# W_out column sums by 64x32 tiles of TensorE, and batch 0 by column halves, in a fused attention and MLP kernel

## The chip, the core and the metric

The kernel runs on one core of one Trainium2 chip. The metric is the device time of one launch in microseconds (us), the median of several runs on the same chip. Engines are named as in the profile: PE is TensorE's matmul stream (PEld its weight loads), DVE is VectorE, ACT is ScalarE, POOL is GpSimd and SP is SyncE. POOL and SP issue the DMA transfers here. PSUM is the memory that PE writes into; DVE and ACT read it out ("evacuate" it).

## What is computed

Two attentions in a row, then a two-layer MLP. For each of 8 batches and 8 heads, 32 packed queries p attend over 576 keys; their result serves as both keys and values for the 576 queries q. The 8 heads of 64 are put side by side to give x, 4608 rows of 512.

```python
# q, k, v: (8, 8, 576, 64)   p: (8, 8, 32, 64)   all float32
def sm_attn(qq, kk, vv):
    s = scale * np.matmul(qq, kk.transpose(0, 1, 3, 2))
    s = s - np.max(s, axis=-1, keepdims=True)
    a = np.exp(s)
    a = a / (np.sum(a, axis=-1, keepdims=True) + 1e-09)
    return np.matmul(a, vv)
p_packed = sm_attn(p, k, v)
out = sm_attn(q, p_packed, p_packed)
# x: (4608, 512)   w_in: (512, 2048)   w_out: (2048, 512)   s, b: one number each
h = x @ w_in
r = np.maximum(h, 0.0)
g = s * (r * r) + b
return (g @ w_out).astype(np.float32)
```

Since g = s r² + b, the result is s (r² @ w_out) plus b times the column sums of w_out. The kernel computes r² @ w_out and the column sums apart, and joins them when a result tile leaves PSUM.

## The kernel before

A batch of 576 columns goes through these steps, each a function and, in the written order, a short word (the numbers behind a word are the batch and a part of the work):

- `k`, `kh`, `kf`, `q`, `qh`, `v`, `p`, `win`, `wout`: loads. Nearly all go through POOL's queue in the order in which they are written; batch 0's first half of k comes through SP in f32 and is cast by DVE and ACT (`kc`).
- `pT` (`prep_p`), `kT` (`prep_k`, by half of the heads), `qT` (`prep_q`, by half of the heads): transposes on PE into PSUM, copied out by DVE and, for half of q, ACT. From batch 3 on k and q are transposed by DMA on SP's queue (`qo`, `qD`, `kD`).
- `s` (`first_scores`, two words): the scores of p against k, and their exp on ACT (tile e1). `a` (`packed`, two words): exp times v, and the row sums; then DVE writes ppc (the packed result), rd (the reciprocal) and rs.
- `c` (`second_scores`): 16 products of ppc with q, and two exps on ACT (tile e2). `w` (`weights`, two words): the sums of e2 over the packed queries by a product with block ones, ln on ACT (tile ld), exp(-ln) on ACT (tile rcd), and a DVE product that gives the attention weights aT.
- `e` (`packed_w1`, four words) or `E` (`packed_w`, two words): ppc times W_in, scaled by rd, gives pw. The MLP's first layer is then only pw times aT, so attention's second product is never formed. Of an `e` word ACT scales one half and DVE the other.
- `m` (`mlp_in`, 16 words): four products of pw and aT (128x288 each), relu on ACT (tile rlu), square on DVE (into gT).
- `t` (`Out.step(2)`): two of the 16 accumulating products of gT with W_out of one result tile y. At a tile's last step DVE forms s·y + biasrep (tile ysb), and SP's queue stores it.

Batches 0 to 2, and batch 3 up to its weights, follow a list of words written out by hand (ORDER, lines 15 to 29). Every engine keeps its instructions in that order; PE, ACT and DVE each run through their own queue and wait for one another by semaphores. The remaining batches run in a loop of 16 steps (line 682 on) in which one m and several products of the batch before alternate.

PSUM gives four large buffers at first, in two rings of two (`ring`, line 89); the function `big()` takes the next one and waits until it has been evacuated. The word `four` (line 620) takes the two buffers of one ring for good: their four halves hold the three result tiles y[0], y[1], y[2] and the bias sum, and from there on `big()` has two buffers. The word `three` (line 625) gives up all of these and divides PSUM anew: three large buffers and two result tiles.

The column sums of W_out (`bias_part`, line 499) are 16 products of a 128x128 block of ones with W_out, accumulated in the fourth half, two at a time as the words b.0 to b.7; DVE multiplies them by b into biasrep. The lines:

```python
for m in range(m0, m1):
    mm(bps, onesb[:], w_out_sb[:, m, :], start=(m == 0), stop=(m == NFF - 1))
```

`mm` and `tr` (lines 92 to 96) wrap every matmul and transpose, and all DVE, ACT, POOL and SP instructions go through one helper (line 104). The profile's lines L93, L96 and L104 are these helpers, so its rows are told apart by tile names and not by lines.

Of the kernel before, what the change touches and what calls it, by code (L numbers as in the profile page):

```python
# [7 lines left out]
F32 = mybir.dt.float32  # L8
BF16 = mybir.dt.bfloat16
AF = mybir.ActivationFunctionType  # L10
ALU = mybir.AluOpType
# [1 line left out]


ORDER = """
kf kh.0.1 p.0.1 kc v.0 mask kT.0.0 qh.0.0 qh.0.1 pp2.0.1 kT.0.1 pT.0 win.0 s.0.0 s.0.1 a.0.0 win.2
qT.0.0 qT.0.1 p.1.2 a.0.1 c.0 w.0.0 e.0.0 win.1 win.3 wout.0 k.1 w.0.1 e.0.1 q.1 wout.1 e.0.2 m.0.3
pp2.1.2 m.0.0 e.0.3 wout.2 m.0.7 m.0.1 m.0.12 m.0.15 m.0.10 m.0.5 m.0.2 v.1 m.0.14 sb four b.0
kT.1.0 t.2 kT.1.1 t.1 m.0.4 qT.1.0 wout.3 b.1 qT.1.1 t.2 b.2 m.0.6 m.0.13 b.3 m.0.11 k.2 q.2 p.2.8
pT.1 t.0 t.1 t.0 b.4 s.1.0 t.1 s.1.1 t.2 m.0.8 b.5 a.1.0 m.0.9 a.1.1 b.6 t.0 c.1 b.7 t.0 t.1 q.3  # L20
kT.2.0 e.1.0 t.2 t.1 w.1.0 pp2.2.8 v.2 t.1 k.3 t.0 w.1.1 qT.2.1 t.0 t.1 t.0 t.0 e.1.1 t.2 kT.2.1 t.2
t.1 t.2 t.2 m.1.0 m.1.3 v.3 three t.3 t.3 pT.2 e.1.2 m.1.2 qT.2.0 t.3 t.3 m.1.1 m.1.5 m.1.7 t.3
e.1.3 m.1.9 qo.3 qD.3 kD.3 s.2.0 t.3 t.4 k.4 m.1.14 pT.3 t.4 m.1.4 s.2.1 t.3 m.1.13 m.1.15 m.1.6
m.1.8 t.4 m.1.11 m.1.10 m.1.12 a.2.0 t.4 t.4 t.3 a.2.1 t.4 t.4 c.2 t.5 t.4 t.5 q.4 E.2.0 t.6 t.5
w.2.0 t.6 w.2.1 s.3.0 t.5 pT.4 t.6 t.6 vo.3 s.3.1 t.5 t.5 m.2.2 m.2.3 t.6 E.2.1 m.2.1 t.6 t.5 v.4
a.3.0 t.5 m.2.5 a.3.1 t.6 m.2.0 t.7 m.2.15 qo.4 t.7 m.2.4 m.2.9 t.7 qD.4 m.2.7 t.7 c.3 t.7 t.6 m.2.6
kD.4 m.2.14 m.2.10 m.2.13 t.7 w.3.0 t.8 t.7 t.8 E.3.0 t.8 t.7 t.8 w.3.1 t.8 E.3.1 t.8 m.2.11 vo.4
t.8 t.8 m.2.12 m.2.8
"""

@with_exitstack
def kernel(
# [21 lines left out]
    B, H, S, D = q.shape  # L54
    NP = p.shape[2]
    DM = H * D
    DFF = moe_w_in.shape[1]
    P = 128
    scale = 1.0 / float(D) ** 0.5

    R = 96
    NC = S // R
    CP = NC // 2
    HP = H // 2
    NQ = H // 4
    NKC = DM // P
    NFF = DFF // P
    NB = 512
    NCH = DFF // NB
    HS = S // 2  # L70
# [21 lines left out]
    def mm(*a, **kw):  # L92
        return tc.keep_in_program_order(nc.tensor.matmul(*a, **kw))  # L93

    def tr(*a, **kw):
        return tc.keep_in_program_order(nc.tensor.transpose(*a, **kw))  # L96
# [11 lines left out]
    def big(dt=F32):  # L108
        w = NB if dt == F32 else 2 * NB
        rings["n"] += 1  # L110
        ps = rings["h"][rings["n"] % len(rings["h"])]
        return ps.tile([P, 2, w], dt, tag="h", name="hps")
# [10 lines left out]
    def raw(name, b):  # L123
        if (name, b - 1) in mine and b > 3:
            mine[name, b] = mine[name, b - 1]
        else:
            mine[name, b] = spare.pop(0)
        return bufs[mine[name, b]][:]
# [7 lines left out]
    def done(name, b):  # L136

        halves[name, b] = halves.get((name, b), 0) + 1
        if halves[name, b] == 2:
            give(name, b)  # L140
# [9 lines left out]
    def load_pairs(store, src, b, tag, half):  # L150

        if half == 0:
            store[b] = raw(tag, b).rearrange("r (h x) -> r h x", h=H)
        for h2 in range(2):
            h0 = HP * h2 + 2 * half
            pool.dma_start(
                out=store[b][:, h0:h0 + 2, :],
                in_=src[b, h0:h0 + 2].rearrange("h (r c) d -> r h (c d)", c=NC),
            )

    w_in_sb = wpool.tile([P, NKC, DFF], BF16, name="w_in_sb")
    w_out_sb = wpool.tile([P, NFF, NB], BF16, name="w_out_sb")
    gT = wpool.tile([P, NFF, 3 * S], BF16, name="gT")
# [51 lines left out]
    vec.memset(onesbd[:], 0.0)  # L215
    for g in range(4):
        vec.memset(onesbd[NP * g:NP * g + NP, NP * g:NP * g + NP], 1.0)
    onesb = constp.tile([P, P], BF16, name="onesb")
    vec.memset(onesb[:], 1.0)
    onesf = constp.tile([P, P], F32, name="onesf")  # L220
    vec.memset(onesf[:], 1.0)
    biasrep = constp.tile([P, NB], F32, name="biasrep")

    def idle(n):
# [60 lines left out]
    def prep_q(b, half):  # L285

        i = b % 2
        tp = big(BF16)
        for x in range(2):
            hp = 2 * half + x  # L290
            for c in range(NC):
                for h2 in range(2):
                    tr(
                        tp[D * h2:D * h2 + D, x, c * R:(c + 1) * R],
                        qn[b][:, hp + HP * h2, c * D:(c + 1) * D],
                        identb[0:R, 0:R],
                    )
        for x in range(2):
            dst = qT[i][:, :, 2 * half + x, :]
            src = tp[:, x, 0:S].rearrange("p (c r) -> p c r", c=NC)  # L300
            if x == 0:
                act.copy(out=dst, in_=src)
            else:
                vec.tensor_copy(out=dst, in_=src)
        done("qn", b)
# [107 lines left out]
    def weights(b, qd):  # L413
# [8 lines left out]
        act.activation(out=rcd[:], in_=ld[:].rearrange("p a s -> p (a s)"), func=AF.Exp, scale=-1.0)  # L422
        vec.tensor_tensor(out=aT[b][:, qd, :], in0=e2[b][:, qd, :], in1=rcd[:], op=ALU.mult)

    def packed_mm(i, ch, outs):

        for hp in range(HP):
            for h2 in range(2):
                mm(
                    outs[h2][NP * hp:NP * hp + NP, :],  # L430
                    ppc[i][D * h2:D * h2 + D, hp, :],
                    w_in_sb[D * h2:D * h2 + D, hp, ch * NB:(ch + 1) * NB],
                    start=True,
                    stop=True,
                    tile_position=(D * h2, NP * hp),
                )
# [32 lines left out]
    def slot(b):  # L469
        return 1 if b % 2 else (b % 4)  # L470
# [5 lines left out]
    def mlp_in(b, m, on_act=True):  # L476
        hps = big()
        for qd in range(NQ):
            for hf in range(2):
                mm(  # L480
                    hps[:, hf, 0:HS],
                    pw[b][:, qd, m * P:(m + 1) * P],
                    aT[b][:, qd, hf * HS:(hf + 1) * HS],
                    start=(qd == 0),
                    stop=(qd == NQ - 1),
                )
        g0 = slot(b) * S
        dst = gT[:, m, g0:g0 + S].rearrange("p (a s) -> p a s", a=2)
        if on_act:
            rlu = ysp.tile([P, 2, HS], BF16, tag="rlu", name="rlu")  # L490
            act.activation(out=rlu[:], in_=hps[:, :, 0:HS], func=AF.Relu)
            vec.tensor_tensor(out=dst, in0=rlu[:], in1=rlu[:], op=ALU.mult)
        else:
            vec.scalar_tensor_tensor(
                out=dst, in0=hps[:, :, 0:HS], scalar=0.0, in1=hps[:, :, 0:HS],
                op0=ALU.max, op1=ALU.mult,
            )

    def bias_part(bps, m0, m1):
        for m in range(m0, m1):  # L500
            mm(bps, onesb[:], w_out_sb[:, m, :], start=(m == 0), stop=(m == NFF - 1))
        if m1 == NFF:
            vec.tensor_scalar_mul(out=biasrep[:], in0=bps, scalar1=bvec[:])

    def sum_w_out(x):

        d = slice(NB // 8 * x, NB // 8 * (x + 1))
        vec.tensor_reduce(
            out=biasrep[:, d], in_=w_out_sb[:, :, d].rearrange("p m d -> p d m"),
            axis=mybir.AxisListType.X, op=ALU.add,  # L510
        )

    def bias_sum():

        bps = big()[:, 0, :]
        mm(bps, onesf[:], biasrep[:], start=True, stop=True)
        vec.tensor_scalar_mul(out=biasrep[:], in0=bps, scalar1=bvec[:])

    def store(ysb, i0, b, col, n, d=slice(0, NB), queues=(sp,)):
# [91 lines left out]


    y = outs(0) + outs(1) + outs(2)
    bias = {}

    def bias_step(x):

        bias_part(bias["ps"], 2 * x, 2 * x + 2)

    def four():  # L620
        ya, yb = (ring[1].tile([P, 2, NB], F32, tag="h", name="yps") for _ in range(2))
        y[0].yps, y[1].yps, y[2].yps, bias["ps"] = (t[:, x, :] for t in (ya, yb) for x in range(2))
        rings["h"] = ring[0:1]

    def three():
# [10 lines left out]
    def constants():  # L636
        sp.dma_start(out=svec[:], in_=moe_s[0:1].unsqueeze(0).to_broadcast([P, 1]))
        sp.dma_start(out=bvec[:], in_=moe_b[0:1].unsqueeze(0).to_broadcast([P, 1]))

    words = {  # L640
        "k": lambda b: load(kn, k, b, "kn"),
        "q": lambda b: load(qn, q, b, "qn"),
# [1 line left out]
        "kh": lambda b, x: load(kn, k, b, "kn", 4 * x, 4 * x + 4),  # L644
        "qh": lambda b, x: load_pairs(qn, q, b, "qn", x),
        "vh": lambda b, x: load_pairs(vn, v, b, "vn", x),
        "kf": load_first_k,
        "kc": cast_first_k,
        "p": lambda b0, b1: load_p(b0, min(b1, B)),
# [7 lines left out]
        "pp2": lambda b0, b1: twice_p(b0, min(b1, B)),  # L657
        "pT": prep_p,
        "kT": prep_k,
        "qT": prep_q,  # L660
        "kD": dma_k,
        "qo": order_q,
        "qD": dma_q,
        "vo": order_v,
        "s": first_scores,
        "a": packed,
        "c": second_scores,
        "w": weights,
        "e": packed_w1,
        "E": packed_w,  # L670
        "m": lambda b, m: mlp_in(b, m),
        "n": lambda b, m: mlp_in(b, m, False),
        "t": lambda t: y[t].step(2),
        "b": bias_step,
        "r": sum_w_out,
        "bs": bias_sum,
    }
    for word in ORDER.split():
# [3 lines left out]
    for b in range(3, B):  # L682
        a = b + 1
# [62 lines left out]
```

## Time and profile before

| | |
|---|---|
| median of 7 runs | 259.06 us (258.80 to 259.52) |
| the profiled execution: its time, its span | 258.96 us, 257.2 us |
| PE busy (share of the span), instructions | 237.1 us (92%), 2283 |
| DVE busy | 144.0 us (56%) |
| ACT busy | 145.0 us (56%) |
| POOL busy | 31.3 us (12%) |
| DMA, moved | 34.61 MB, mean 135 GB/s |
| PE busy in 0 to 25 us | 12.6 of 25 us |
| PE busy in 25 to 40 us | 13.7 of 15 us |
| PE busy in 40 to 100 us | 59.1 of 60 us |
| rlu (ACT), 128 instructions | 651 ns each |
| gT (DVE), 128 instructions | 457 ns each |
| pw of 512 columns, DVE / ACT | 750 / 684 ns each |
| first pw scaling of batch 0; its last gT square | starts at 22.14 us; at 46.43 us |

Times within the execution count from the span's start. "Busy" of PE is the union of its matmuls, each from its start to its modelled end; matmuls are pipelined, so the next one starts before the last has ended, and the time that a group costs is read from its start to the start of the next group. The bytes are counted as written: most loads read f32 and write bf16.

### The profile page before, as it was taken

Reading aid. Unit: us, or ns where it says so; the run is one execution under the profiler, and the core shown is the slowest. Engines: PE = TensorE matmul, PEld = TensorE weight load, DVE = VectorE, ACT = ScalarE, POOL = GpSimd, SP = SyncE. Lnnn points to the kernel's source line nnn. Section 1 sums busy time; section 2 is a strip of 40 time slices with the busy share of each in tenths; the row PEclk is TensorE's granted clock in tenths of the full one; section 3 lists DMA queues with packets and bytes.
Section 4 is the critical chain, followed back from the end, with each engine's and each line's share of the span. In section 5 each row is a group of like instructions: output and inputs, shape, how many; then the busy total and the mean of one; then the engine's idle time right before and its main releaser. Section 6 shows DMA issues by size and latency. Waiting matters only on the chain.

```text
span 257.2 us, 5569 instructions
## 1 busy us (share of the span) xinstructions
PE 237.1 (92%) x2283; PEld 138.0 (54%) x2320; DVE 144.0 (56%) x299; ACT 145.0 (56%) x220; POOL 31.3 (12%) x47
## 2 busy tenths in 40 slices
PE   1477889999999999999999999999999999999994
PEld 1362556555655664665566456655565555555443
DVE  3324753576765877857854668366835473444212
ACT  3038936456848688848763674568554764444000
POOL 8366230110002100300030003000000000000000
PEclk9999999999999999999999999999999999999999
DMA  5999999999398969993979398946611113111332
GB/s 110 183 203 204 204 206 205 197 200 247 71 161 131 176 133 162 157 233 81 186 99 219 99 177 122 235 90 133 136 43 41 43 41 87 41 41 41 84 82 82
DMA packets 54858, 34.61 MB, mean 135 GB/s; under 512 B 27568, under 2 KB 50352, under 8 KB 54832
## 3 DMA queue, kind: packets, MB, share of 16 engines
q0 software_dynamic: 24864, 18.32, 48.2%
q1 hardware_dynamic: 29872, 15.87, 27.3%
q8 instruction: 18, 0.29, 0.5%
q14 instruction: 8, 0.07, 0.1%
q10 hardware_dynamic: 96, 0.07, 0.1%
HBM read 37.23 MB, written 9.44 MB: 181 GB/s over the span
## 4 chain that ended last, share of the span: by engine, by line
PE 82%; DMA 13%; issue 2%; POOL 1%; ACT 1%; DVE 0%; ACTq 0%; POOLq 0%
PE yps L93 48%; PE hps L93 32%; DMA w_out_sb<-in_moe_w_out_dram 6%; DMA raw<-in_v_dram 4%; DMA w_in_sb<-in_moe_w_in_dram 3%; PE hps L96 1%; POOL raw L104 1%; ACT rlu L104 1%; DVE gT L104 0%; DVE ysb L104 0%; POOL pn L104 0%; ACTq L104 0%; POOLq L730 0%
## 5 line engine op out<-in xcount | busy, mean ns | idle before, releaser
L93 PE MATMUL yps<-w_out_sb,gT 128*128 128x512 bf16 (+2 forms) x558 | 138.3, 373 | 2.7 <-issue 1.4
L104 ACT ACTIVATE rlu<-hps 128x576 bf16<-128x576 f32 x128 | 80.7, 651 | 63.5 <-PE hps L93 57.6
L104 DVE TENSOR_TENSOR gT<-rlu 128x576 bf16<-128x576 bf16 x128 | 58.1, 457 | 62.1 <-ACT rlu L104 60.2
L93 PE MATMUL hps<-aT,pw 128*128 128x288 bf16 x512 | 81.0, 289 | 0.6 <-DVE pw L104 0.4
L93 PEld LDWEIGHTS <-gT 128*128 128x128 bf16 x592 | 53.2, 98 | 48.6 <-issue 6.4
L93 PEld LDWEIGHTS <-pw 128*128 128x128 bf16 x512 | 49.6, 98 | 34.1 <-issue 1.1
L104 DVE SCALAR_TENSOR_TENSOR ysb<-yps,svec,biasrep 128x512 f32<-128x512 f32 (+2 forms) x37 | 27.0, 732 | 16.6 <-PE yps L93 16.5
L104 DVE TENSOR_SCALAR pw<-hps,rd 128x1024 bf16<-128x1024 f32 (+1 forms) x20 | 21.3, 1067 | 1.9 <-ACT pw L104 1.4
L104 ACT ACTIVATE pw<-hps,rd 128x1024 bf16<-128x1024 f32 (+1 forms) x20 | 18.7, 941 | 4.1 <-PE hps L93 3.3
L104 DVE TENSOR_TENSOR aT<-e,rcd 128x576 bf16<-128x576 bf16 x16 | 12.1, 758 | 13.1 <-ACT rcd L104 13.1
L96 PE MATMUL hps<-identb,raw 96*64 96x96 bf16 (+1 forms) x216 | 9.9, 232 | 8.7 <-DVE raw L104 5.7
L104 POOL DMA_DIRECT2D raw<-in_k_dram x8 | 6.3, 790 | 93.3 <-DMA kT<-raw 83.7
L104 ACT ACTIVATE e<-hps 96x768 bf16<-96x768 f32 x16 | 12.6, 800 | 8.3 <-PE hps L93 8.3
L104 ACT ACTIVATE e<-hps,rs 128x576 bf16<-128x576 f32 x16 | 10.9, 737 | 6.4 <-PE hps L93 6.4
L96 PEld LDWEIGHTS <-raw 96*64 96x64 bf16 (+1 forms) x216 | 8.5, 123 | 11.1 <-DVE raw L104 5.7
L93 PE MATMUL hps<-w_in_sb,ppc 64*32 64x512 bf16 x256 | 11.8, 404 | 1.0 <-DMA w_in_sb<-in_moe_w_in_dram 1.0
L104 ACT ACTIVATE rcd<-ld 128x576 f32<-128x576 f32 x16 | 10.9, 683 | 0.5
L104 ACT ACTIVATE ld<-hps 128x576 f32<-128x576 f32 x16 | 10.3, 646 | 1.2 <-PE hps L93 1.0
L104 DVE COPY raw<-raw 96x1536 bf16<-96x1536 bf16 x20 | 10.4, 562 | 0.0
L93 PEld LDWEIGHTS <-raw 96*64 96x64 bf16 (+1 forms) x264 | 8.4, 113 | 2.9 <-issue 2.1
L93 PE MATMUL hps<-e,raw 96*64 96x32 bf16 (+1 forms) x264 | 9.1, 193 | 0.8 <-ACT e L104 0.8
L93 PE MATMUL hps<-pbd,kT 128*128 128x64 bf16 x192 | 8.6, 199 | 1.1 <-DVE pbd L104 1.1
(41 smaller groups left out, 97.1 us busy)
## 6 DMA issues: line engine op xcount, KB each, us to landing
raw<-in_v_dram POOLq DMA_DIRECT2D x8, 576.0 KB, 11.8
out_dram<-ysb SPq DMA_DIRECT2D x23, 192.0 KB, 2.6
raw<-in_k_dram POOLq DMA_DIRECT2D x7, 576.0 KB, 6.7
raw<-in_q_dram POOLq DMA_DIRECT2D x7, 576.0 KB, 10.5
out_dram<-ysb SPq DMA_DIRECT2D x24, 128.0 KB, 2.5
w_in_sb<-in_moe_w_in_dram POOLq DMA_DIRECT2D x8, 256.0 KB, 8.8
w_out_sb<-in_moe_w_out_dram POOLq DMA_DIRECT2D x4, 512.0 KB, 16.6
out_dram<-ysb SPq DMA_DIRECT2D x23, 64.0 KB, 2.2
```

The lines of the kernel that those rows point to most:

```text
L93: return tc.keep_in_program_order(nc.tensor.matmul(*a, **kw))
L96: return tc.keep_in_program_order(nc.tensor.transpose(*a, **kw))
L104: return lambda *a, **kw: tc.keep_in_program_order(f(*a, **kw))
```

## The change

- The words `b` go. In their place one word `B` (`sums_w_out`) forms all sums at one point: for each of 16 blocks of W_out and each half of the partitions one product of a 64x32 block of ones with 64 rows of W_out, on one of eight tiles of the array. 32 products leave partial sums in four groups of 32 partitions and two halves of one large buffer. DVE copies one half into biasrep and adds the other.
- The word `bs` (`bias_sum`, which was there and unused) forms one f32 product of biasrep with a 128x128 block of 1/32 (`parts`, which was `onesf`, a block of 1), and DVE multiplies by b.
- `four` gives the fourth half to y[3], so four result tiles of batch 0 are open.
- Batch 0 goes by column halves of 288: `prep_q_chunks`, `second_scores_half`, `weights_half` and `mlp_in_half` take 288 columns of all heads, or of two blocks of the MLP, where the old functions take 576 columns of half the heads, or of one block. The number of products and their sizes stay the same; the exps of batch 0's second scores are four of 288 columns in place of two of 576.
- Batch 0's W pieces, and one of batch 1, become `f` words: `packed_w1` with both halves on DVE.
- ORDER is written anew in all its lines. Four words `z` (one product of zeros, 128x512) stand near its start.

```diff
-kf kh.0.1 p.0.1 kc v.0 mask kT.0.0 qh.0.0 qh.0.1 pp2.0.1 kT.0.1 pT.0 win.0 s.0.0 s.0.1 a.0.0 win.2
-qT.0.0 qT.0.1 p.1.2 a.0.1 c.0 w.0.0 e.0.0 win.1 win.3 wout.0 k.1 w.0.1 e.0.1 q.1 wout.1 e.0.2 m.0.3
...
+kf kh.0.1 qh.0.0 mask kT.0.1 p.0.1 z kc z pp2.0.1 z qh.0.1 z kT.0.0 pT.0 v.0 qT.0.1 s.0.0 s.0.1
+qT.0.0 a.0.0 win.0 win.1 a.0.1 c.0.0 win.2 f.0.0 w.0.0 c.0.1 f.0.1 p.1.2 q.1 wout.0 w.0.1 h.0.2
+win.3 sb f.0.2 h.0.0 wout.1 k.1 h.0.4 h.0.3 h.0.8 h.0.6 h.0.10 h.0.1 h.0.9 four wout.2 pp2.1.2
+qT.1.0 t.1 h.0.5 t.0 t.1 t.2 t.2 h.0.7 t.3 wout.3 t.0 v.1 f.0.3 k.2 t.3 q.2 t.0 h.0.11 h.0.15 t.3
+h.0.14 t.2 t.3 t.1 h.0.12 t.0 kT.1.0 qT.1.1 t.3 t.2 pT.1 p.2.8 t.3 kT.1.1 B t.2 t.1 t.2 h.0.13 t.1
+k.3 s.1.0 s.1.1 t.1 t.3 bs t.1 a.1.0 kT.2.1 q.3 a.1.1 t.3 c.1 t.1 pp2.2.8 t.2 w.1.0 qT.2.0 t.2 w.1.1
+t.0 t.0 e.1.0 t.0 v.2 qT.2.1 t.0 m.1.0 three pT.2 kT.2.0 v.3 e.1.1 m.1.2 m.1.1 f.1.2 m.1.5 t.5 e.1.3
+m.1.3 t.4 m.1.8 m.1.4 t.4 qo.3 m.1.7 m.1.9 m.1.10 m.1.13 t.4 qD.3 m.1.15 m.1.6 m.1.14 s.2.0 t.5
+s.2.1 m.1.11 t.4 m.1.12 t.4 a.2.0 pT.4 kD.3 a.2.1 t.4 t.4 c.2 pT.3 t.4 t.5 E.2.0 t.5 w.2.0 k.4 t.5
...
-    onesb = constp.tile([P, P], BF16, name="onesb")
+    onesb = constp.tile([P, 32], BF16, name="onesb")
-    onesf = constp.tile([P, P], F32, name="onesf")
-    vec.memset(onesf[:], 1.0)
+    parts = constp.tile([P, P], F32, name="parts")
+    vec.memset(parts[:], 1.0 / 32)
...
+    def weights_half(b, hf):
+        cols = slice(hf * HS, (hf + 1) * HS)
+        dps = big()
+        for qd in range(NQ):
+            mm(dps[:, qd, 0:HS], onesbd[:], e2[b][:, qd, cols], start=True, stop=True)
...
+    def mlp_in_half(b, x):
+        mp, hf = divmod(x, 2)
+        hps = big()
+        for y in range(2):
+            m = 2 * mp + y
+            for qd in range(NQ):
+                mm(
+                    hps[:, y, 0:HS],
+                    pw[b][:, qd, m * P:(m + 1) * P],
+                    aT[b][:, qd, hf * HS:(hf + 1) * HS],
...
+    def sums_w_out():
+        t = big()
+        for g in range(4):
+            for x in range(4):
+                for h2 in range(2):
+                    mm(
+                        t[32 * x:32 * x + 32, h2, :],
+                        onesb[D * h2:D * h2 + D, :],
+                        w_out_sb[D * h2:D * h2 + D, 4 * g + x, :],
+                        start=(g == 0),
+                        stop=(g == 3),
+                        tile_position=(D * h2, 32 * x),
+                    )
+        vec.tensor_copy(out=biasrep[:], in_=t[:, 0, :])
+        vec.tensor_tensor(out=biasrep[:], in0=t[:, 1, :], in1=biasrep[:], op=ALU.add)
...
-        mm(bps, onesf[:], biasrep[:], start=True, stop=True)
+        mm(bps, parts[:], biasrep[:], start=True, stop=True)
...
-        y[0].yps, y[1].yps, y[2].yps, bias["ps"] = (t[:, x, :] for t in (ya, yb) for x in range(2))
+        for i in range(4):
+            y[i].yps = (ya, yb)[i // 2][:, i % 2, :]
```

The lines of ORDER that are left out follow batch 2 and the start of batch 3, with the same words as before in another order.

## The prediction

> **What bounds the kernel now.** First the page: of a span of 257.2 us the matrix engine (PE) is busy 92%, and the chain of work that ended last is PE's:
>
> ```profile
> PE 82%; DMA 13%; issue 2%; POOL 1%; ACT 1%; DVE 0%; ACTq 0%; POOLq 0%
> ```
>
> The 13% of DMA lies in the first 38 us (v, then w_in, then w_out). Then the timeline, for where PE becomes the bound (start, us, instructions; in brackets the idle time before and what ended it):
>
> ```profile
> 5.70 1.14 PE L96 MATMUL hps<-identb,raw 96*128 96x96 bf16 x12 [5.70 <-DVE raw L104]
> ...
> 9.27 1.14 PE L96 MATMUL hps<-identb,raw 96*128 96x96 bf16 x12 [2.43 <-DMA raw<-in_k_dram]
> ...
> 11.76 1.44 PE L93 MATMUL hps<-pbd,kT 128*128 128x64 bf16 x24 [1.13 <-DVE pbd L104]
> ...
> 18.66 0.68 PE L93 MATMUL hps<-qT,ppc 64*32 64x288 bf16 x16 [0.56 <-DVE ppc L104]
> ...
> 24.54 2.10 PE L93 MATMUL hps<-aT,pw 128*128 128x288 bf16 x8
> ...
> 31.46 0.38 PE L93 MATMUL yps<-w_out_sb,onesb 128*128 128x512 bf16 x1
> ```
>
> Until 24.5 us PE waits; from 31.3 us (its weight load) it hardly does. It also starts at half speed: eight MLP products take 2.10 us at 24.54 and 1.14 at 57.77 (below); the first full-speed group starts at 26.57. The stretch that the new order rewrites:
>
> ```profile
> 47.27 0.51 PE L93 MATMUL hps<-qT,ppc 64*32 64x288 bf16 x16
> ...
> 57.77 1.14 PE L93 MATMUL hps<-aT,pw 128*128 128x288 bf16 x8
> ...
> 72.75 0.56 PE L93 MATMUL hps<-e,raw 96*64 96x32 bf16 x24
> ```
>
> These are c.1 (batch 1's second scores), m.1.0 and a.2.0; I use them as marks. What ScalarE (ACT) needs per softmax step, from its timeline:
>
> ```profile
> 76.90 1.37 ACT L104 ACTIVATE e<-hps,rs 128x576 bf16<-128x576 f32 x2 [3.28 <-PE hps L93]
> ...
> 80.04 0.65 ACT L104 ACTIVATE ld<-hps 128x576 f32<-128x576 f32 x1
> 80.72 0.68 ACT L104 ACTIVATE rcd<-ld 128x576 f32<-128x576 f32 x1
> 81.31 0.63 ACT L104 ACTIVATE ld<-hps 128x576 f32<-128x576 f32 x1
> 81.98 0.69 ACT L104 ACTIVATE rcd<-ld 128x576 f32<-128x576 f32 x1
> 82.57 1.48 ACT L104 ACTIVATE e<-hps 96x768 bf16<-96x768 f32 x2
> ```
>
> Start to start these cost 0.6 to 0.7 us each. PE's costs, likewise start to start at full speed: a t step (two 128x512 products) 0.43, an m or h word (four 128x288) 0.49, eight w_in tiles 0.34, a k half 0.6, a q half 0.58.
>
> **Work removed and added.** Sixteen 128x512 products with ones (0.216 each) go: -3.46 us of PE. In come 32 products of 64x32 tiles. The same shape runs 16 in 0.56 us at 98.92 and 8 in 0.41 at 49.62, so 1.12 to 1.64; I take 1.12, the longer run. The f32 product has no row. Bounds: 0.22, as the bf16 row of its shape, and 0.86, if each of the two operands, twice as wide, doubles it; I take 0.86. Net -1.5 us. DVE gets a copy and an add (0.75 each, as its f32 row biasrep) ahead of the old 0.75 scaling; t.2, t.1, t.2 and h.0.13 (2.2 us of PE) cover them before s.1.0 needs that PSUM buffer, so nothing. Without the cover it would be 1.5. The Trainium skill (FP8 and Floating Point Precision, TensorE Precision Notes) has an f32 product make four passes; by that it would be an estimate of 0.86 as well, but no run here shows it yet.
>
> **The start, to 31 us.** Loads on POOL's queue: q now goes ahead of v, w_in in order 0, 1, 2, then p, q of batch 1, w_out 0, w_in 3, w_out 1, k of batch 1. The bytes are the same, and k's second half (issued 1.28, landing 7.9 us later) comes first in both. By the old landings v moves from 12.3 to about 15, and k of batch 1 from 32 to about 36; the new order reaches its users at 16.9 and 41.5, so these cost nothing. Batch 0's p is issued behind two q loads and the mask (0.66, 0.66 and 0.32 on POOL), some 1.6 us later; it landed at 9.4 and is not used before 12.9. But k's second half is now transposed first. DVE's cast of the first half (5.08 before) queues behind the kT copy (0.76) that waits for it: 9.25 + 0.93 + 0.2 + 0.76 = 11.2, cast to 11.75. The four zero products (0.43 each at half speed, 1.7) run in just that gap. Then by the old half-speed rows: k half 11.9 to 12.9, p, a q half to 14.2, pbd copies to 14.45, scores to 15.85, q half to 16.85 (its exps end 16.85), a.0.0 and a.0.1 to 19.0, ppc and reciprocal, c.0.0 at 19.5, 0.85 us later than before. The halves pay it back: two exps of 288 (an estimate of 0.45 each, from 0.65 for 576 and 0.94 for 1024 columns), ld 0.65, rcd 0.68, so the first aT is ready at 23.8 where 24.5 was the first MLP product. Nine h words then run at DVE's and ACT's pace: DVE has all eight pw scalings of batch 0 (0.7 each; ACT did four), ACT 0.59 per h. The word four, with qT.1.0 behind it, comes at 31.05, against 31.34. At that point 9 of 16 products and 3 of 4 W pieces are done, before 10 and 4: 0.49 + 0.34 = 0.83 us still owed.
>
> **From there to a.2.0.** Before: 72.75 - 31.34 = 41.4 us. By the rows PE's own work in it is 16 bias products 3.46, 34 t steps 14.7, 22 m 10.8, four W pieces 1.36, four k halves 2.5, four q halves 2.3, scores, packing, second scores and weights of batches 1 and 2 3.9: 39.05, so 2.35 of stalls. After: 39 t steps at the same mark, as t.3 opens early in the old bias slot. Own work 39.05 + 5 x 0.43 - 1.5 + 0.83 - 0.1 (one p fewer) = 40.45. The stalls are what decides. I followed each queue by hand with the durations above. Up to c.1: 0.25 and 0.4 where h.0.5 and h.0.15 wait for a PSUM buffer, 0.4 at c.1, where ppc and the reciprocal queue on DVE behind the kT.2.1 copy and one t step stands between, where two did: 1.0. From c.1 to pT.2: ACT needs two exps, ld, rcd, a q copy, ld, rcd, pw, a q copy and one rlu, 10 x 0.65 plus handing over, while PE has 7 t steps, two q halves, two weights, one W piece and m.1.0: 5.5 us in all; before there were 15 t steps there. PE waits at qT.2.0, e.1.0, m.1.0 and, 0.85, at pT.2: the word three gives up all PSUM, so it needs m.1.0's rlu, and before the t.3 steps stood in between. Together 2.0. In batch 1's MLP, with 7 t steps for 10, DVE has three pw pieces ahead of the gT squares that t.4 waits for: 1.0. Sum 4.0 of stalls.
>
> So a.2.0 comes at 31.05 + 40.45 + 4.0 = 75.5. The old kernel had the same work done at 72.75 + 5 x 0.43 = 74.9. Difference +0.6 us. Behind it batch 2 has ACT work of 23 us under 29 of PE, the loop of batches 3 to 7 is unchanged, and both end alike: nothing. The profiled execution took 258.96 (span 257.2, 1.8 around it), 0.1 below the median: 259.6.
>
> **The clock, the largest unknown.** Half speed until 26 us is the assumption above. PE is now nearly without a gap from 9.25 to 19 us, with 1.7 us of dense products in it. Before it ran so from 14.15 to 18.11, at half speed still at 18.66; from 23.56 to 26.5 it ran dense products and came up. So the rows leave open whether transposes and narrow products bring it up. The Trainium skill (TensorE: Matmul & The Clock Gate, Part 4) says that transposes do not count as PE activity in the same way, which speaks against an early rise, and in Part 1 that a window of some 3.4 us must be busy; by this the zero products are too few and the sum stays at 259.6, while the row at 18.66 fits either.
>
> **Rivals.** (1) The clock rises by about 16 us. Then scores, q half and a.0 take 1.1 us less and the first h words 0.65 less; four comes at 29.3, and everything behind moves with it: 259.6 - 1.75 = 257.9. For it: the gapless stretch; against: 18.66. (2) The stalls do not come, because ACT's hand-overs are quicker than I count: 2.35 as before in place of 4.0, 258.0 at half speed, 256.2 with (1). Against: ten ACT steps in a row. (3) Still slower: the h words, waiting for DVE at 26 to 30 us, leave PE too idle to come up there, where before it was busy 4.63 of 5 us. If half speed lasts until 34, three us of work cost 1.5 more: 261.1. It decides if PE's share between 25 and 30 falls well below that 4.63. (4) W_out's sums at their upper bound, 0.5 more, lie within the forecast's range; the f32 product at 0.22 takes 0.64 off.
>
> **Numbers.** Forecast as summed (half speed, stalls by hand, each way 0.8): chance 0.52, of which slower 0.32, same 0.15, faster 0.05. Rival 1: 0.30 (faster 0.27, same 0.03). Rival 2: 0.07, faster. Rival 3: 0.11 (slower 0.10, same 0.01). So faster 0.39, same 0.19, slower 0.42, where same is within 0.2% (0.52 us), about what a measurement of this kernel can tell. The forecast's own range is 258.8 to 260.4; the 8 in 10 reaches to rival 1 and part of rival 3: 257.6 to 260.9.
>
> **What would show it.** Right, step by step: c.0.0 near 19.5 with half-speed products; qT.1.0 near 31; PE gaps of some 0.4 to 0.9 at qT.2.0, e.1.0, m.1.0 and pT.2, ended by ACT or DVE; c.1 near 54; a.2.0 near 75.5; the tile sums in about 1.1 us, the f32 product in 0.9. Wrong: full-speed products before 18 us (rival 1), no gap between c.1 and pT.2 (rival 2), a PE wait on a load in front of a.0.0, f.0.0 or kT.1.0, which I priced at nothing, or half-speed rows beyond 31 us (rival 3).

## The result, and the profile after

The changed kernel takes 257.31 us (median of 13 runs, 256.48 to 258.13), the kernel before 259.11 us in the same session (32 runs, 258.64 to 259.52). The ratio is 0.9933, 95% interval 0.9925 to 0.9941: 1.8 us faster, where 0.6 us slower was forecast. The profiled execution has a span of 255.5 us against 257.2.

On the page the chain that ended last is PE's once more, and the DMA share in it has fallen from 13% to 3%:

```profile
PE 86%; ACT 4%; DMA 3%; DVE 3%; issue 2%; ACTq 0%; POOLq 0%
```

The timeline of PE after the change, with the same marks as before (start, us, instructions; in brackets the idle time before and what ended it):

```profile
8.90 1.14 PE L96 MATMUL hps<-identb,raw 96*128 96x96 bf16 x12 [8.90 <-DMA raw<-in_k_dram]
9.84 1.91 PE L93 MATMUL hps<-zeros 128*128 128x512 bf16 x4
...
14.06 0.87 PE L93 MATMUL hps<-pbd,kT 128*128 128x64 bf16 x24 [0.34 <-DVE pbd L104]
...
18.04 0.32 PE L93 MATMUL hps<-qT,ppc 64*32 64x288 bf16 x8 [0.38 <-DVE ppc L104]
...
20.80 0.63 PE L93 MATMUL hps<-w_in_sb,ppc 64*32 64x512 bf16 x7 [0.67 <-DMA w_in_sb<-in_moe_w_in_dram]
...
22.12 1.16 PE L93 MATMUL hps<-aT,pw 128*128 128x288 bf16 x4
...
29.41 0.70 PE L96 MATMUL hps<-identb,raw 96*64 96x96 bf16 x24
...
43.00 1.06 PE L93 MATMUL hps<-w_out_sb,onesb 64*32 64x512 bf16 x32
...
47.89 1.02 PE L93 MATMUL hps<-biasrep,parts 128*128 128x512 f32 x2
48.75 0.59 PE L93 MATMUL yps<-w_out_sb,gT 128*128 128x512 bf16 x2
...
51.70 0.51 PE L93 MATMUL hps<-qT,ppc 64*32 64x288 bf16 x16
...
58.20 0.65 PE L93 MATMUL hps<-aT,pw 128*128 128x288 bf16 x4
59.59 0.27 PE L96 MATMUL hps<-identb,pn 128*128 128x128 bf16 x2 [0.74 <-ACT rlu L104]
...
73.20 0.56 PE L93 MATMUL hps<-e,raw 96*64 96x32 bf16 x24
```

Read it by stretches. The first scores take 0.87 us at 14.06, where the same 24 products took 1.44 before: the clock was up, from 13.2 us on, 13 us earlier than the prediction assumed. c.0.0 stands at 18.04 (forecast 19.5), qT.1.0, the mark of the word four, at 29.41 (31.05), c.1 at 51.70 (near 54), a.2.0 at 73.20 (75.5). The granted clock fell again in between, as the table of windows shows (stretch, its length, then the busy time of PE, PEld, DVE, ACT, POOL with counts, then the granted clock, the DMA share and GB/s):

```profile
18.00:20.00 2.00, 1.41 (x27) 0.45 (x28) 1.69 (x4) 1.17 (x3) 1.00 (x2) 1.00 1.24 206
20.00:27.00 7.00, 6.22 (x36) 3.01 (x35) 5.15 (x10) 5.01 (x9) 3.04 (x4) 0.51 1.31 203
27.00:32.00 5.00, 4.95 (x55) 3.41 (x54) 3.68 (x10) 4.55 (x8) 2.40 (x4) 1.00 1.24 205
```

So h.0.2 at 22.12 took 1.09 us from its start to the next (0.49 at full speed). The record of the granted clock reads 1.00 until its first change, also where products run at half speed: in the kernel before it reads 1.00 from 12 to 13 us, where the scores take 1.44 us. A mean of 0.98 for an execution therefore tells of a clock that came up early and fell again; a mean of 1.0 tells of one that came up late, or came up and stayed.

ACT's work from c.1 to pT.2, which the prediction counted as ten steps in a row:

```profile
52.27 1.37 ACT L104 ACTIVATE e<-hps,rs 128x576 bf16<-128x576 f32 x2 [4.01 <-PE hps L93]
...
57.65 0.64 ACT L104 COPY qT<-hps 128x576 bf16<-128x576 bf16 x1 [0.38 <-PE hps L96]
58.88 0.65 ACT L104 ACTIVATE rlu<-hps 128x576 bf16<-128x576 f32 x1 [0.60 <-PE hps L93]
```

It is one chain almost without a gap until 57.3, and its last step, m.1.0's rlu, ends at 59.53; pT.2 starts at 59.59.

**Where the time came from.** Split the span at qT.1.0 (before: at 31.34, the weight load of the first bias product). Before: 31.34 + 225.86. After: 29.41 + 226.09. So 1.93 us were gained ahead of the mark and 0.23 lost behind it, although the W_out sums are cheaper there by 1.6. Two things qualify this. At the mark the changed kernel has done 0.83 us less of batch 0's work (9 of 16 products and three of four W pieces, where the kernel before had 10 and four); like for like the start gained 1.1 us and the part behind the mark 0.6. And without the cheaper sums the new order does not pay at all (e2). The experiments are read by this split, because the first part also varies between executions (k's second half lands anywhere from 8.9 to 10.0 us). The table has each profiled execution; "k" is the first transpose of k's second half.

| kernel | k | qT.1.0 | k to qT.1.0 | span behind it |
|---|---|---|---|---|
| before (mark 31.34) | 9.27 | 31.34 | 22.07 | 225.86 |
| after | 8.90 | 29.41 | 20.51 | 226.09 |
| after, again (e9) | 9.49 | 30.34 | 20.85 | 226.06 |
| e1 no zero products | 9.14 | 29.35 | 20.21 | 226.05 |
| e2 old column sums | 9.59 | 30.45 | 20.86 | 227.95 |
| e4 m.1.0 behind three | 9.76 | 29.86 | 20.10 | 226.64 |
| e5, e10 pauses filled | 9.80, 9.24 | 29.56, 29.05 | 19.76, 19.81 | 226.04, 226.15 |
| e6 one more pw on ACT | 9.85 | 31.03 | 21.18 | 226.37 |
| e7 no column halves | 9.24 | 30.35 | 21.11 | 226.05 |
| e8 three tiles open | 9.55 | 30.77 | 21.22 | 228.73 |
| e12 filled, pw on ACT | 9.95 | 28.99 | 19.04 | 226.31 |
| e13 first half first | 9.15 | 29.10 | 19.95 | 226.30 |
| e14 e13, pw on ACT | 9.13 | 30.29 | 21.16 | 226.61 |
| e15 e14, pauses filled | 8.97 | 28.50 | 19.53 | 226.60 |

Where an edit leaves the words behind the mark alone, the last column is 226.0 to 226.3 in eight profiled executions, but 226.6 in e14 and e15. The 1.9 us of e2 and the 2.6 of e8 lie clear of that; the 0.55 of e4 and the 0.3 of e6 do not by this column alone.

### The profile page after: what moved, and what is told of

Read it like the earlier page. It is cut to its first block, busy times and chain, and to the rows that moved or that the text cites. A ratio compares the mean times of both kernels' runs of the same rounds, so it can differ in the third digit from the quotient of the medians.

```text
span 255.5 us, 5624 instructions
## 1 busy us (share of the span) xinstructions
PE 236.5 (93%) x2307; PEld 137.3 (54%) x2342; DVE 147.8 (58%) x306; ACT 141.8 (56%) x217; POOL 31.4 (12%) x47
## 4 chain that ended last, share of the span: by engine, by line
PE 86%; ACT 4%; DMA 3%; DVE 3%; issue 2%; ACTq 0%; POOLq 0%
PE yps L93 47%; PE hps L93 37%; DMA raw<-in_k_dram 3%; PE hps L96 2%; ACT e L104 2%; ACT rlu L104 1%; DVE pw L104 1%; DVE aT L104 1%; ACT rcd L104 1%; ACT ld L104 0%; DVE ysb L104 0%; DVE kT L104 0%; ACT pw L104 0%; DVE pbd L104 0%; DVE gT L104 0%
## 5 line engine op out<-in xcount | busy, mean ns | idle before, releaser
L93 PE MATMUL hps<-aT,pw 128*128 128x288 bf16 x512 | 82.2, 291 | 0.3
L93 PEld LDWEIGHTS <-pw 128*128 128x128 bf16 x512 | 50.2, 99 | 33.4 <-issue 1.5
L104 DVE TENSOR_SCALAR pw<-hps,rd 128x512 bf16<-128x512 f32 (+1 forms) x25 | 24.6, 1002 | 0.8 <-PE hps L93 0.3
L96 PE MATMUL hps<-identb,raw 96*64 96x96 bf16 (+1 forms) x216 | 9.3, 218 | 9.1 <-DMA raw<-in_k_dram 8.9
L104 ACT ACTIVATE pw<-hps,rd 128x1024 bf16<-128x1024 f32 (+1 forms) x15 | 15.4, 1026 | 2.9 <-PE hps L93 2.9
L104 ACT ACTIVATE e<-hps,rs 128x576 bf16<-128x576 f32 (+1 forms) x18 | 11.3, 683 | 8.6 <-PE hps L93 8.4
L96 PEld LDWEIGHTS <-raw 96*64 96x64 bf16 (+1 forms) x216 | 8.0, 113 | 11.4 <-DMA raw<-in_k_dram 8.9
L104 DVE COPY kT<-hps 128x1152 bf16<-128x1152 bf16 x6 | 4.5, 757 | 10.0 <-PE hps L96 9.9
L93 PEld LDWEIGHTS <-ppc 64*32 64x32 bf16 x384 | 4.0, 89 | 9.7 <-issue 7.6
```

The source lines that it names most:

```text
L104: return lambda *a, **kw: tc.keep_in_program_order(f(*a, **kw))
```

## Experiments

All but e3 and e11 are edits of the changed kernel, and every ratio is to the kernel before on the same chip.

**e1: without the four zero products.**

```diff
-kf kh.0.1 qh.0.0 mask kT.0.1 p.0.1 z kc z pp2.0.1 z qh.0.1 z kT.0.0 pT.0 v.0 qT.0.1 s.0.0 s.0.1
+kf kh.0.1 qh.0.0 mask kT.0.1 p.0.1 kc pp2.0.1 qh.0.1 kT.0.0 pT.0 v.0 qT.0.1 s.0.0 s.0.1
```

> The changed kernel without its four zero products (z); nothing else differs. Theory: dense products are needed to bring the clock up before 14 us, so the first scores (24 products) take 1.44 us again in place of 0.87, c.0.0 starts near 19.3 in place of 18.04, the word four (first q transpose of batch 1) comes near 30.8 in place of 29.4, and the time is near 258.7. Rival A: the transposes alone are activity enough, c.0.0 stays at 18.0, and the time stays at 257.3. Rival B: the gain is only the smaller W_out sums, the clock does not matter, 257.3 whatever c.0.0 does.

Measured: 257.57 us (12 runs, 257.03 to 259.20), ratio 0.9951 [0.9935, 0.9968]. PE's timeline:

```profile
14.09 1.46 PE L93 MATMUL hps<-pbd,kT 128*128 128x64 bf16 x24
15.48 1.07 PE L96 MATMUL hps<-identb,raw 96*64 96x96 bf16 x24
16.39 0.64 PE L93 MATMUL hps<-e,raw 96*64 96x32 bf16 x24
```

The scores run at half speed (1.46), a.0.0 nearly at full: the clock rose near 16 us with transposes and narrow products alone, and qT.1.0 (29.35) stands where it stood with the zero products. That is rival A, with c.0.0 at 18.37. Nine of the 12 executions have a mean granted clock of 0.984 to 0.987, as the changed kernel's have (0.980 to 0.987), and a median of 257.26; three have 0.999 to 1.0, like the kernel before, and 258.23, 258.45 and 259.20. I read these three as executions without an early rise (no profile of one exists): then the zero products bring in all 25 executions of the changed kernel (here and in e9) what comes three times in four without them, and the early rise is worth about 1.2 us in this order of the start, by three executions only (two of the nine, 258.17 and 258.51, are as slow).

**e3: zero products in the kernel before.** Eight words z near the start of its ORDER: five behind kT.0.0, two behind pT.0, one behind s.0.1.

> The kernel before with eight zero products: five after the first k half, two after the p transposes, one after the first scores, all where PE was idle. Theory: the clock rises near 13 us here too; scores, q halves and packing run at full speed, c.0 starts near 17.5 in place of 18.66, and as w_in's arrival then bounds the W pieces, half of it is lost: near 258.3. Rival: the rise comes only with the new order's longer run without gaps, or w_in's arrival hides all of it: 259.1.

Measured: 259.05 (12 runs), ratio 0.9998 [0.9988, 1.0007]. Half of the executions show a clock of 0.974 to 0.980, so by the reading above an early rise and some 10 us or more at half speed behind it (10.2 us gave 0.980 in the profiled execution of e6); the others show 0.999 to 1.0. Both take the same time (medians 259.02 and 259.05), and the theory fell: an early clock that falls again bought nothing in the old order. Why is not shown. The MLP there waits for loads (in the profiled execution, which did not rise early, for w_in at 22.64, 0.48 us, and 23.87, 0.63), but the later fall may as well cost what the early rise gains, and no execution with an early rise was profiled.

**e13: the start of the order before.** The first half of k is cast and transposed first, the zero products are gone.

```diff
-kf kh.0.1 qh.0.0 mask kT.0.1 p.0.1 z kc z pp2.0.1 z qh.0.1 z kT.0.0 pT.0 v.0 qT.0.1 s.0.0 s.0.1
+kf kh.0.1 qh.0.0 mask kc kT.0.0 p.0.1 pp2.0.1 qh.0.1 kT.0.1 pT.0 v.0 qT.0.1 s.0.0 s.0.1
```

> The changed kernel with the start of the order before: the first half of batch 0's k is cast and transposed first (kc, kT.0.0), the second when it lands (kT.0.1), and the four zero products are gone, so that TensorE stands between the two as it did before. Theory (the prediction's start failed because the clock rises at 13 us in the changed kernel, and only in the dense stretch that the new start makes): half-speed products in all of a.0 and c.0.0, a full clock in no execution before 20 us, the mean clock at 0.998 to 1.0 as in the runs of before, qT.1.0 at 30.3 to 31.0 in place of 29.4 to 30.3, and 258.2 to 259.0. Rival (the clock comes up as early without that stretch, or the earlier start of the work makes up for it): a clock of 0.980 to 0.987 in most executions and 257.0 to 257.6.

Measured: 257.12 (5 runs, 256.99 to 257.52), ratio 0.9928 [0.9914, 0.9941], clock 0.998 to 1.0 in all. PE's timeline:

```profile
11.33 1.55 PE L96 MATMUL hps<-identb,raw 96*64 96x96 bf16 x24
12.82 1.46 PE L93 MATMUL hps<-pbd,kT 128*128 128x64 bf16 x24
...
17.85 0.44 PE L93 MATMUL hps<-qT,ppc 64*32 64x288 bf16 x8 [0.38 <-DVE ppc L104]
...
22.14 1.16 PE L93 MATMUL hps<-aT,pw 128*128 128x288 bf16 x4
```

Half of the theory held: there was no early rise, and h.0.2 at 22.14 still runs at half speed (the clock came up at 26.2). Its price did not come: qT.1.0 at 29.10, and the time of the changed kernel. The scores start at 12.82 instead of 14.06, which makes up for 1.46 in place of 0.87. So the early clock is not the source of the gain. The second half first, with the zero products, costs about what the clock that it brings repays. What both starts share, against before (the same half speed, c.0 at 18.66): q is transposed ahead of a.0.0, half of it ahead of the scores, where PE had stood 1.13 us; before, all of it stood between a.0.0 and a.0.1. To this I put down the 0.8 us up to c.0.0 (0.1 of it is the earlier k). From there to the mark it is 11.25 us, before 12.68, with these waits in the kernel before:

```profile
22.32 0.61 PE L93 MATMUL hps<-w_in_sb,ppc 64*32 64x512 bf16 x1 [0.34 <-DMA w_in_sb<-in_moe_w_in_dram]
23.56 1.05 PE L93 MATMUL hps<-w_in_sb,ppc 64*32 64x512 bf16 x15 [0.63 <-DMA w_in_sb<-in_moe_w_in_dram]
...
28.75 2.87 PE L93 MATMUL hps<-aT,pw 128*128 128x288 bf16 x22 [0.37 <-DVE pw L104]
```

Of the 1.43 us between them 0.83 is the work that this order does only behind the mark. Against the rest stand shorter waits: PE is idle for 2.19 us of that stretch before, for 1.33 in the changed kernel and for 0.64 here. No run takes q's order, the loads and the W pieces one by one, so this part of the account is argued and not shown.

**e7: no column halves at c.** `c.0.0 win.2 f.0.0 w.0.0 c.0.1 f.0.1` becomes `c.0.0 c.0.1 win.2 f.0.0 w.0.0 f.0.1`.

> c.0.1 stands directly behind c.0.0, ahead of win.2, f.0.0 and w.0.0, so that batch 0 isn't run by column halves at c, only its work in two parts. Theory (the first half's aT, f and w come earlier by the halves, which brings MLP 0 forward): w.0.0 0.6 to 0.9 us later than 19.02, qT.1.0 by as much (30.0 to 30.3) and 257.9 to 258.2. Rival (the run of MLP 0 is set by what comes last, w.0.1 and the loads of w_in, which the order of the halves doesn't move): qT.1.0 at 29.4 and 257.3.

Measured: 258.22 (6 runs, 257.37 to 258.52), ratio 0.9964 [0.9950, 0.9978]. Inconclusive: the median is 0.9 above, but w.0.0 moved by 0.54 us (19.56), of which 0.34 is the later k, and k to qT.1.0, 21.11, is that of e6 and e8, which keep the halves and had, like this execution, a granted clock of 0.980.

**e5, e10 and e9: PE's pauses filled, and the changed kernel again.**

```diff
+    def fill(t, n):
+        for x in range(n):
+            mm(t[:, 0, 0:HS], zeros[:, 0:P], zeros[:, 0:HS], start=True, stop=True)
 # c.0.0: fill(t, 3)   w.0.0: fill(dps, 3)   w.0.1: fill(dps, 5)   f.0.1: fill(t, 4)
```

> The changed kernel with zero products added: three of 288 columns into each PSUM tile of c.0.0 and of w.0.0, five into that of w.0.1, four into that of f.0.1, all of them ahead of the group's own products (start=True), where TensorE stood for 0.3 to 1.4 us. They compute nothing that is kept. Theory (the first products of batch 0's MLP ran at half speed because TensorE stood too long between 14 and 20 us): the granted clock stays at 1.0 from 13.3 us on, h.0.2 takes 0.6 instead of 1.16 us, the 32 products of the h run 3.5 to 4.5 instead of 5.50, qT.1.0 stands at 28.2 to 28.6 instead of 29.41, and the time is 256.3 to 256.7. Rival: ScalarE and VectorE, who evict those tiles, set the pace of the run, so the products run faster and wait as much more: qT.1.0 at 29.3 to 29.5 and 257.3. A second rival: the added products themselves delay c.0.0 or w.0.0 by 0.3 to 0.5 us: 257.6 to 257.8.

> The kernel with the 15 added zero products of the experiment on the clock, now on one chip with the changed kernel. Theory (the half-speed stretch behind 18 us, whose length differs between executions, costs the changed kernel its spread and some of its time): clock 1.0 in every execution, times within 0.5 us of each other, and a median 0.3 to 1.0 below the changed kernel's of the same chip. Rival (ScalarE and VectorE set the pace of batch 0's MLP, and the clock is nearly free): within 0.2 of the changed kernel's median.

> The changed kernel once more, for comparison on this chip with the two kernels that fill TensorE's pauses. Both theories: 257.3, with single executions between 256.5 and 258.5, which lie the higher the longer TensorE ran at half speed behind 18 to 20 us (6.7 or 10.2 us in the executions seen so far, granted clocks of 0.987 and 0.980).

Measured: e5 257.23 (5 runs, 256.93 to 257.41), ratio 0.9933 [0.9921, 0.9944]. On another chip, together: e10 256.93 (5 runs, 256.65 to 257.02), ratio 0.9919 [0.9907, 0.9932]; the changed kernel (e9) 257.31 (12 runs, 256.63 to 258.83), ratio 0.9942 [0.9926, 0.9958]. PE in e10:

```profile
22.40 0.65 PE L93 MATMUL hps<-aT,pw 128*128 128x288 bf16 x4
22.98 0.73 PE L93 MATMUL hps<-w_in_sb,ppc 64*32 64x512 bf16 x8
...
26.50 2.62 PE L93 MATMUL hps<-aT,pw 128*128 128x288 bf16 x20 [1.03 <-DVE pw L104]
29.05 0.70 PE L96 MATMUL hps<-identb,raw 96*64 96x96 bf16 x24
```

The granted clock is 0.997 to 1.0 in all ten executions, h.0.2 takes 0.58 us to the next start, and k to qT.1.0 shrinks from 20.51 and 20.85 to 19.8. Most of what the products save becomes a wait for DVE's pw (1.03 us at 26.50). So e5 came out by its first rival. e10 met its theory, if barely: 0.38 us less in the median, with ratios whose intervals overlap, and 0.37 us of spread instead of 2.2. A part of the changed kernel's spread goes with the clock: the two slowest of e9's 12 runs (258.66, 258.83) have a granted clock of 0.980. The other ten, at 0.984 to 0.987, still spread from 256.63 to 258.19.

**e12, e14, e15: that pw on ACT.** `f.0.2` becomes `e.0.2`: in e12 on top of the fill, in e14 on e13, in e15 on e13 with six zero products (1, 1, 2, 2) in the pauses.

> The kernel with the added zero products, and one word more changed: f.0.2 becomes e.0.2, so that the power of that part of batch 0 is evicted by ScalarE and not by VectorE, which stood behind the aT of the second half and held TensorE for 0.82 us at 26.2 to 27.0. Theory (with the clock kept, VectorE's queue is what is late): the wait is cut by 0.5 to 0.8 us and the time is as much below that of the kernel with the zero products alone, 256.4 to 256.8. Rival (ScalarE's relu of the MLP words queue behind that power and hold TensorE's PSUM tiles for the same time): no gain, 257.2, or 0.3 more.

> The start of the order before (first half of k first, no zero products) as in the experiment before this one, and f.0.2 made e.0.2: that power on ScalarE. Theory (with the start's extra work gone, VectorE's queue is what batch 0's MLP waits for next: its pw at 24.82 to 26.22 stands ahead of the squares): qT.1.0 at 28.4 to 28.8 in place of 29.10, 256.4 to 256.9. Rival (at half speed TensorE itself sets the pace of the first products, so that the eviction isn't late): 29.1 and 257.1.

> The same with six zero products of 288 columns in TensorE's pauses (one before c.0.0, one before w.0.0, two before f.0.1, two before w.0.1). Theory (the pauses of 17 to 23 us keep the clock down until 24.2 us; filled, it comes up one stretch of 3.4 us earlier, near 20.8): the first h words at full speed, qT.1.0 at 27.8 to 28.4 and 256.0 to 256.6. Rival (the clock stays down as without them, and the added products, 0.24 us each at half speed, delay what follows): 257.1 to 257.8.

Measured: e12 257.01 (5 runs), ratio 0.9927 [0.9915, 0.9939]; e14 257.61 (6 runs, 256.52 to 258.70), 0.9944 [0.9924, 0.9964]; e15 256.97 (6 runs), 0.9922 [0.9907, 0.9937]. In e12 the wait of 1.03 us became 0.44, and k to qT.1.0 the shortest of all, 19.04, but k landed at 9.95 in that execution and the median did not follow. The profiled execution of e14 is its slowest; PE waited 0.67 us for v at 16.11 there, which was not so in e13. e15 reached qT.1.0 first of all, at 28.50 (its clock came up at 23.5, that of e13 at 26.2, where the expectation had read 24.2), then waited for W_out (0.20 at 29.41), with 0.5 more behind. None of the three theories got its time, and all stay within 0.4 us of the changed kernel. That loads decide once batch 0's MLP is earlier would fit these waits; it is not shown.

**e2: the old column sums in the new order.** B becomes 16 products of 128x128 ones and bs nothing.

> The changed kernel with the column sums formed by 16 products with a 128x128 block of ones at the place of B, and bs left empty; all else as changed. Theory: PE is the bound there, so its own work counts in full: 16 x 0.216 = 3.46 us against the measured 0.99 + 0.86, so +1.6 us, near 258.9. Rival: the work hides in waits that the new order has anyway (0.4 at c.1, 2 to 3 us up to batch 1's MLP), less than +0.8, below 258.1.

Measured: 259.97 (12 runs, 258.47 to 261.63), ratio 1.0040 [1.0017, 1.0063]. PE's timeline:

```profile
43.94 3.62 PE L93 MATMUL hps<-w_out_sb,onesb 128*128 128x512 bf16 x16
47.40 1.46 PE L93 MATMUL yps<-w_out_sb,gT 128*128 128x512 bf16 x6
...
54.24 0.51 PE L93 MATMUL hps<-qT,ppc 64*32 64x288 bf16 x16
...
62.55 0.27 PE L96 MATMUL hps<-identb,pn 128*128 128x128 bf16 x2 [1.16 <-DVE ysb L104]
```

From the start of the sums to c.1 it takes 10.30 us against 8.70: +1.6, the theory's term to the digit. Behind c.1 pT.2 waits 0.4 longer, so 1.9 in all behind qT.1.0; the other 1.0 of the profiled 2.9 lies ahead of the mark, which this edit doesn't touch. With the old sums in one run at this place the new order is slower than the kernel before, so the cheaper sums are a condition of the gain.

**e11: the new sums alone in the kernel before.** b.0 to b.7 are gone, B stands at b.7's place, bs ahead of w.1.0.

> The kernel before with only the W_out sums of the change: its 16 products of ones (b.0 to b.7) are gone, the 32 products of 64 by 32 tiles (B) stand where b.7 stood, behind c.1, and the f32 product (bs) some words later, ahead of w.1.0; three tiles of W_out sums are open as before. Theory (the sums are work on TensorE's path, worth the 1.5 us net that the prediction worked out, in either order): 257.4 to 257.8. Rival (in the order of before the products of ones fill pauses in which TensorE waits for transposes' loads and evictions, among 31 and 47 us, so part of them was free): 258.3 to 258.8.

Measured: 260.60 (7 runs, 260.08 to 263.64), ratio 1.0081 [1.0048, 1.0114]: 1.6 us slower, worse than either expectation. PE's timeline:

```profile
45.88 0.51 PE L93 MATMUL hps<-qT,ppc 64*32 64x288 bf16 x16 [0.38 <-DVE ppc L104]
47.25 1.06 PE L93 MATMUL hps<-w_out_sb,onesb 64*32 64x512 bf16 x32 [0.85 <-ACT e L104]
```

Between kT.1.0 and c.1 twelve products of ones are gone, 2.6 us at 0.216, but that stretch is only 1.6 shorter (13.57 against 15.14): the missing 1.0 is time in which they had filled pauses, such as the 0.38 ahead of c.1. And B needs a whole large buffer, where the old sums sat in their own: behind c.1 it waits 0.85 us for ACT's exp to give one up. From c.1 to a.2.0 it is 28.07 us, 25.48 before.

**e4: m.1.0 behind the barrier.** `m.1.0 three pT.2 kT.2.0` becomes `three pT.2 kT.2.0 m.1.0`.

> The changed kernel with the word m.1.0 moved behind three, pT.2 and kT.2.0. Theory: the 0.74 us in which PE waits at pT.2 for m.1.0's relu comes from three, which needs every PSUM buffer back; with m.1.0 behind it the gap shrinks to 0.2 or less and the time falls to about 256.8. Rival: DVE is the bound from 55 to 65 us (9.3 of 10 us busy), so the wait only moves to m.1.2, and the time stays at 257.3.

Measured: 258.53 (12 runs, 257.70 to 259.51), ratio 0.9978 [0.9962, 0.9993]. PE at pT.2:

```profile
60.04 0.27 PE L96 MATMUL hps<-identb,pn 128*128 128x128 bf16 x2 [1.44 <-DVE ysb L104]
```

pT.2 stands 30.18 us behind qT.1.0, as in the changed kernel; the wait has doubled, because m.1.0 no longer fills it. From pT.2 to a.2.0, where m.1.0 now runs, it takes 14.18 us against 13.61: that is the edit's price, 0.57 (the rest of the 1.2 in the median is not explained by it). The theory fell: the barrier opens no earlier than DVE's queue has got through its ysb, and the rlu that the profile names in the changed kernel is only the last by a hair (DVE's last ysb there ends at 59.43, the rlu at 59.53).

**e6: one pw of batch 1 on ACT.** `f.1.2` becomes `e.1.2`.

> One word of the order changed: f.1.2 becomes e.1.2, so that the power of that part of batch 1 is evicted by ScalarE and not by VectorE, in the stretch where VectorE was busy 4.69 and 4.63 of 5 us (55 to 65). Theory (VectorE's queue sets pT.2 and what follows there): 0.3 to 0.5 us less from qT.1.0 to a.2.0 (43.3 to 43.5 instead of 43.8) and 256.8 to 257.0. Rival (pT.2 is released before that word's work begins, or ScalarE becomes as late as VectorE): 43.8 and 257.3, or up to 0.5 more.

Measured: 257.65 (9 runs), ratio 0.9956 [0.9940, 0.9972]. The rival held: the gain did not come; in the profiled execution, the slowest of the nine, the part behind qT.1.0 is 0.3 longer and pT.2 waits 1.05 instead of 0.74 (unedited words there vary as much: see e14 in the table).

**e8: three tiles open.** `four` opens y[0] to y[2], and all eight t.3 move behind `three`.

> Only three column tiles of W_out sums of batch 0 are open before the barrier of batch 1: the word four opens y[0] to y[2], and all eight t.3 move behind the word three, one or two between each of its words up to m.1.8. Theory (the eight sums of tile 3, 1.7 us of work, were missing behind three, where pT.2 waited 0.74 and later MLP words 1.0 together): the stalls behind three go (-1.2 to -1.7), the stretch from qT.1.0 to c.1 gets 0.3 to 0.8 of them back as waits for P or loads: 256.3 to 257.0. Rival (the stretch before c.1 has no slack, so that it stands for the 1.7 us that are taken from it): c.1 at the same 22.3 us behind qT.1.0, everything behind it 1.7 later less the stalls saved: 257.5 to 258.5.

Measured: 260.71 (5 runs), ratio 1.0064 [1.0051, 1.0077]. PE's timeline:

```profile
59.51 1.02 PE L79 MATMUL yps<-w_out_sb,gT 128*128 128x512 bf16 x4 [0.64 <-DVE ysb L90]
...
68.94 0.59 PE L79 MATMUL yps<-w_out_sb,gT 128*128 128x512 bf16 x2 [0.97 <-DVE ysb L90]
```

Up to c.1 it takes 20.95 us, 1.34 less, for the 1.7 that were moved: 0.36 came back as waits, as the theory said, and the rival's c.1 at the same 22.3 fell. But the stalls behind three did not go: t.3 now takes one of the two result buffers there, and its steps and those of the next tiles wait for DVE's ysb. The part behind the mark is 2.6 longer. Both expectations were too low.

## Why the prediction was wrong

The direction was wrong by two terms, which add up: 259.6 - 1.64 - 0.65 = 257.3. With the 0.83 us that are still owed at the mark, the forecast had the start lose 0.5 us; it gained 1.1.

- **The start (31.05 forecast, 29.41 measured) is the step that failed**, at "half speed until 26 us is the assumption above" and "then by the old half-speed rows ... c.0.0 at 19.5". The clock was up at 13.2 us, and c.0.0 came at 18.04: 1.46 of the 1.64. Of this 0.35 is k's second half, which landed at 8.90 and not at 9.25, and 1.1 the clock, as much as rival 1 gave it. The text bet on half speed because before's row at 18.66 was still slow, and weighed the gapless stretch against it as rival 1, at the lower chance.
- **From c.0.0 to the word four** it said 11.55 and got 11.37, though by another way: half speed was forecast until 26 us; in fact the clock fell at 20.1 and rose at 26.9. That the two agree is luck.
- **The clock is still not why the change pays.** Without the early rise, and with the old order of k's halves, the kernel is as fast (e13). The loss by "k's second half is now transposed first" is real: at half speed the scores start at 14.09 in e1 and at 12.82 in e13, with k at 9.14 and 9.15; the early clock buys it back. The gain that the sum missed lies in the order of the work: q ahead of a.0.0, and shorter waits of PE for w_in and pw on its way to the mark (argued from the rows, see e13).
- **W_out's sums**: -1.5 net forecast, -1.6 measured in the new order: 0.99 for the tiles (forecast 1.12), 0.86 for f32 (forecast 0.86), 3.46 for the old ones. What the term didn't say is that it depends on the order; put alone into the kernel before, at the place of b.7, it is a loss (e11).
- **The stalls** by hand were 4.0; from qT.1.0 to a.2.0 it took 43.8 against a forecast of 44.45, so with the tiles at 0.99 they were 3.5. What was too much lay ahead of c.1, which came 22.3 us behind qT.1.0 where some 22.9 was forecast (c.1 near 54): the waits of 0.25 and 0.4 priced at h.0.5 and c.1 do not show in the rows. From c.1 to a.2.0 it is 21.5, as forecast, with pT.2's wait at 0.74 (0.85). The mechanism held there, and the size of the term was 0.5 too large.
- **Loads at nothing**: in the profiled execution a.0.0 and kT.1.0 waited for none; in those of e4 and e5 a.0.0 waited 0.52 and 0.47 us for v, about as long as it waits for ACT's exp otherwise (0.52). The second W piece waited 0.67 us for w_in (the row at 20.80), but c.0.1's exps kept ACT until 21.87 anyway, and w.0.1 needs them.
- **Rivals**: rival 1 had the mark right (29.3), in part by luck, since the clock fell again and the first h words ran at half speed; its time was 0.6 too high, as it kept the 4.0 of stalls. Rival 3's condition did not come: PE was busy all of the 5 us from 25 to 30, and at full speed from 27.

## What to carry to other kernels

Split a span at a mark, and count the work that each kernel has done at it before the parts are compared: here 0.83 of the 1.93 us gained ahead of the mark had only moved behind it. Work that looks removable may be the filler of a pause, so price a removal by the pauses that it leaves. Before a clock is credited with a gain, run the order that lacks it.

## What the runs showed of the hardware

- The clock fell although PE had short pauses only. In the traces' records its changes lie 3.41 us apart, or two or three times that: up at 13.23, down at 20.06, up at 26.89 in the changed kernel; 16.31, 19.73 and 26.55 in e1; 15.40, 18.81 and 29.05 in the profiled execution of e6. The Trainium skill (TensorE: Matmul & The Clock Gate, Part 1) has a window of about 3.4 us that runs freely and lets the clock fall after an idle one. The lengths agree; an idle one was not needed here. In the 3.41 us ahead of the fall PE was busy 0.72 of the time in the changed kernel and 0.83 in e6, with no pause over 0.52 us, while in the changed kernel 0.75 (13.23 to 16.65) had kept the clock. With fifteen zero products in the pauses the granted clock was 0.997 to 1.0 in ten of ten executions.
- What brings the clock up stays open. In e1 PE was busy from 11.6 us with transposes and narrow products and it rose at 16.3, against what the prediction held for likely; in e13 it was busy with the same kinds from 11.0 to 17.5 (6.36 of the 6.5 us) and did not rise before 26.2.
- 32 products of 64x32 tiles, 512 columns each, take 0.99 us (0.031 each where a 128x128 one takes 0.216), and an f32 product of 128x512 0.86, four times the bf16 one.
